# An attention and MLP-mixer kernel: the second MLP product by seven half products, keys and values pair-summed on the way in, and new step plans

## The chip, the core and the metric

The kernel runs on one core of a Trainium2 chip. A core has five engines that work side by side, each on its own queue of instructions in order: TensorE (PE, with PEld for its weight loads), VectorE (DVE), ScalarE (ACT), GpSimd (POOL) and SyncE (SP). Data move between HBM and the on-chip memory SBUF by DMA; TensorE writes its results into PSUM, eight banks of 128 rows by 2 KB. The time is device microseconds (us) of one execution. The kernel before takes 284.99 us, the median of 3 runs (284.35 to 285.2).

## The reference

Eight batches, eight heads, 576 rows, 64 columns a head (512 in all). Keys and values are averaged over groups of eight rows, so each head has 72 pooled keys. The attention output `x` goes through a token MLP with a residual, then a channel MLP with a residual:

```
k_p = k.reshape(B, H, Sp, pool, D).mean(axis=3)          # v_p likewise; pool = 8, Sp = 72
attn = softmax(scale * q @ k_p.T);  x = attn @ v_p         # -> (B, 576, 512)
h = relu(x.T @ w_tok1) @ w_tok2                            # 576 -> 256 -> 576, along the rows
u = x + h.T
h2 = relu(u @ w_ch1) @ w_ch2                               # 512 -> 1536 -> 512, along the columns
out = u + h2
```

## The kernel before

**Units.** The channel MLP is cut into nine units of 512 rows. Units 0 to 7 hold the first 512 rows of batches 0 to 7 (four chunks of 128); the last 64 rows of every batch are gathered in `u_tails`, and unit 8 takes these. In a unit (`unit_steps`, L439) the first stage makes 12 tiles of `GT` (hidden channels by rows): four matmuls of 512 columns each (L451), then a ReLU on ScalarE (L455). The second stage makes four output chunks: 12 matmuls each of 512 columns, accumulated in one bank (L474), then VectorE adds `u` (L479) and SP stores it (L482). In unit 8 the last chunk is made in two halves of 256 columns (L463).

**Steps.** `unit_steps` is a generator that yields after every two matmuls, 48 steps (0 to 47) a unit, 24 in the first stage. At a yield, `unit` (L515) issues what the plan lists for that step, so that attention work for later batches is woven between the MLP's matmuls. The order on every engine is the order of issue, written out by hand in the plans `FIRST` (unit 0), `SECOND`, `THIRD` and `LATER` (units 3 to 8), L489 to L501. A name alone is for the next batch, `<` for the unit's own batch, `>` for the batch after the next; `l` loads. Before unit 0 stands `HEAD` (L487), the attention of batch 0, in which `d` issues matmuls on zeros that keep TensorE running.

**The names in the plans.** `lk2` loads keys of batch n+2 (`lq`, `lv` likewise): one DMA from POOL's queue that casts float32 to bf16 (L87, L104). `K0`, `K1`, `V0`, `V1` pool half the heads' keys or values on POOL; `k1`, `v1` do it on VectorE: three additions (L146, L147, L150 or L152). `kpT` transposes pooled keys on TensorE and copies them to `kD` on VectorE (L195, L197). `Q0`, `Q1` transpose the queries on VectorE (L244). `s0` to `s3` are scores, eight small matmuls (L255) and two exponentials on ScalarE (L261). `av0` to `av4` make the `x` tiles: eight matmuls (L293), then a reciprocal and a product on VectorE (L305, L311). `at0`, `at1` are the token MLP's first stage, five matmuls (L339) and a ReLU, the first on ScalarE (L330), the second on VectorE (L332). `u0` to `u4` are its second stage and the residual (L354, L355), `t0` to `t4` the transposes of `u` for the next unit (L364, L365). From batch 4 on these transposes go through DRAM instead (`M`, `T`: L373 to L394).

**PSUM.** `ps_one` has three banks (first and second stage, AT, u), `ps_tr` one (transposes), `ps_two` two pairs (scores, x tiles).

## Time and profile before

| | before |
|---|---|
| median of 3 runs | 284.99 us (284.35 to 285.2) |
| the profiled execution | 285.26 us; span 283.5, so 1.76 around it |
| granted TensorE clock | 0.999 |
| head (before the first first-stage matmul) | 0 to 24.95 us |
| units 0, 1, 2 | 34.98, 32.87, 32.50 us |
| units 3, 4, 5, 6 | 28.15, 29.44, 28.59, 26.06 us |
| units 7, 8 (no attention work) | 21.24, 20.92 us |
| last matmul's end to the end of the span | 3.8 us |

The unit times are from one first-stage start (L451) to the next unit's. A line of the groups gives source line, engine, operation, output <- input, shape and count, then busy us, mean ns of one, and the idle time of the engine in front with what ended it. A line of a timeline or of the chain in order of time begins with its start and length in us. Matmuls overlap: their mean duration is longer than the distance from one start to the next, and the distance is what a row of them costs.

### The profile page before, as it was taken

How to read it: one execution, taken by the hardware profiler on the slowest of the kernel's cores; microseconds unless marked ns; L12 is line 12 of the kernel's file. 1: busy time of each engine (PE TensorE's matmuls, PEld its weight loads, DVE VectorE, ACT ScalarE, POOL GpSimd, SP SyncE). 2: the span in 40 equal slices, each digit the busy share in tenths (PEclk: the TensorE clock that was granted, in tenths of full speed). 3: DMA queues.
4: the chain of work that ended last, by engine and by line, in shares of the span. 5: the costliest groups of instructions: out<-in, count | busy, mean ns of one | idle time of the engine just before them, and what ended most of it. 6: DMA issues, size and time to landing. Idle time of an engine off the chain costs nothing.

```text
span 283.5 us, 4515 instructions
## 1 busy us (share of the span) xinstructions
PE 274.8 (97%) x1816; PEld 130.3 (46%) x1816; DVE 138.2 (49%) x265; ACT 110.3 (39%) x193; POOL 140.1 (49%) x124
## 2 busy tenths in 40 slices
PE   8999899999999999999999999999999999999994
PEld 3755335444553544354445443544354444444443
DVE  5466977777583756175247434833383141011012
ACT  2543481029404642604751366046603512612600
POOL 8584894999999939974993796000000000000000
PEclk9999999999999999999999999999999999999999
DMA  7999999960893187159649955325132445015014
GB/s 148 194 202 207 204 205 200 234 135 2 123 166 74 39 118 132 43 96 202 143 90 151 222 139 81 82 58 129 39 76 56 126 78 112 3 37 111 2 39 110
DMA packets 36837, 32.68 MB, mean 115 GB/s; under 512 B 14288, under 2 KB 30288, under 8 KB 36816
## 3 DMA queue, kind: packets, MB, share of 16 engines
q0 software_dynamic: 18672, 17.64, 39.2%
q1 hardware_dynamic: 17984, 14.62, 21.9%
q8 instruction: 14, 0.23, 0.3%
q10 hardware_dynamic: 160, 0.13, 0.2%
q14 instruction: 7, 0.06, 0.1%
HBM read 38.21 MB, written 11.80 MB: 176 GB/s over the span
## 4 chain that ended last, share of the span: by engine, by line
PE 91%; DVE 5%; ACT 2%; issue 1%
PE p L451 31%; PE p L474 31%; PE p L354 6%; PE p L339 5%; PE p L255 4%; PE p L293 3%; PE pt L508 3%; ACT ex L261 2%; PE pt L364 1%; DVE t L146 1%; PE p L463 1%; PE p L273 1%; PE p L322 1%; DVE qD L244 1%; PE p L411 1%; PE p L226 1%
## 5 line engine op out<-in xcount | busy, mean ns | idle before, releaser
L474 PE MATMUL p<-w_ch,GT 128*128 128x512 bf16 x420 | 102.3, 379 | 0.0
L451 PE MATMUL p<-uT,w_ch 128*128 128x512 bf16 x384 | 96.6, 383 | 0.0
L455 ACT ACTIVATE GT<-p 128x512 bf16<-128x512 f32 x108 | 64.3, 596 | 82.4 <-PE p L451 82.4
L451 PEld LDWEIGHTS <-w_ch 128*128 128x128 bf16 x432 | 39.8, 97 | 48.9 <-issue 4.1
L474 PEld LDWEIGHTS <-GT 128*128 128x128 bf16 x420 | 37.6, 98 | 41.4 <-issue 3.7
L261 ACT ACTIVATE ex<-p 72x576 bf16<-72x576 f32 x56 | 33.1, 642 | 26.1 <-PE p L255 26.1
L479 DVE TENSOR_TENSOR o<-p,u 128x512 f32<-128x512 f32 x32 | 21.9, 684 | 36.6 <-PE p L474 36.6
L146 POOL TENSOR_TENSOR t<-kr 72x1024 f32<-72x1024 bf16 x13 | 27.9, 2143 | 23.6 <-DMA kr<-in_k_dram 23.0
L147 POOL TENSOR_TENSOR t<-t 72x512 f32<-72x512 f32 x25 | 33.5, 1339 | 2.0
L355 DVE TENSOR_TENSOR u<-p,x 128x512 bf16<-128x512 f32 x32 | 22.1, 690 | 14.0 <-PE p L354 13.9
L146 POOL TENSOR_TENSOR t<-vr 72x1024 f32<-72x1024 bf16 x12 | 25.5, 2122 | 1.1 <-DMA vr<-in_v_dram 0.4
L311 DVE TENSOR_TENSOR x<-p,den 128x512 bf16<-128x512 f32 x30 | 20.7, 691 | 1.0
L330 ACT ACTIVATE AT<-p 128x512 bf16<-128x512 f32 x8 | 4.8, 597 | 39.4 <-PE p L339 36.6
L293 PEld LDWEIGHTS <-ex 72*128 72x128 bf16 x320 | 15.4, 98 | 9.9 <-DVE x L311 0.8
L354 PE MATMUL p<-AT,w_tok 128*128 128x512 bf16 x64 | 19.0, 378 | 0.0
L387 DVE STREAM_TRANSPOSE uT<-v 128x256 uint32<-128x256 uint32 x16 | 6.1, 419 | 24.6 <-DMA v<-mem 24.6
L293 PE MATMUL p<-vp,ex 72*128 72x65 bf16 x320 | 16.8, 194 | 0.5 <-DVE x L311 0.3
L255 PE MATMUL p<-qD,kD 32*72 32x288 bf16 x224 | 14.4, 298 | 0.7 <-DVE kD L197 0.4
L339 PE MATMUL p<-x,w_tok 128*128 128x512 bf16 x56 | 14.4, 379 | 0.0
L305 DVE RECIPROCAL den<-p 128x8 f32<-128x8 f32 (+1 forms) x39 | 8.0, 204 | 11.5 <-PE p L293 10.9
L150 POOL TENSOR_TENSOR kp<-t 72x256 bf16<-72x256 f32 x13 | 12.1, 928 | 1.0
L332 DVE TENSOR_SCALAR AT<-p 128x512 bf16<-128x512 f32 x8 | 5.5, 691 | 13.9 <-PE p L339 13.1
(88 smaller groups left out, 209.5 us busy)
## 6 DMA issues: line engine op xcount, KB each, us to landing
out_dram<-o SPq DMA_DIRECT2D x70, 128.0 KB, 2.4
kr<-in_k_dram POOLq DMA_DIRECT2D x7, 576.0 KB, 8.3
qb<-in_q_dram POOLq DMA_DIRECT2D x7, 576.0 KB, 11.7
vr<-in_v_dram POOLq DMA_DIRECT2D x7, 576.0 KB, 14.8
w_ch<-in_moe_w_ch_dram POOLq DMA_DIRECT2D x6, 512.0 KB, 13.3
mem<-u SPq DMA_DIRECT2D x8, 256.0 KB, 3.0
v<-mem SPq DMA_DIRECT2D x8, 160.0 KB, 3.8
v<-mem SPq DMA_DIRECT2D x8, 128.0 KB, 3.3
```

What stands on the lines that cost most here:

```text
L146: eng.tensor_tensor(out=t4[:, 0:n], in0=t[:, hs, 0:4], in1=t[:, hs, 4:8], op=ALU.add)
L147: eng.tensor_tensor(out=t4[:, 0:n, 0:2], in0=t4[:, 0:n, 0:2], in1=t4[:, 0:n, 2:4], op=ALU.add)
L255: nc.tensor.matmul(out=pss[l // 2][0:SP, l % 2, 0:SH], lhsT=st["kD"][quad, g, db, :], rhs=st["qD"][quad, g, half * SH:(half + 1) * SH, db] ...
L261: nc.scalar.activation(out=exv[:, h:h + 2], in_=pss[a][0:SP, :, 0:SH], func=AF.Exp, scale=scale)
L293: nc.tensor.matmul(out=halves[h // 4][:, (h % 4) * (D + 1):(h % 4 + 1) * (D + 1)], lhsT=st["ex"][:, h * S + n0:h * S + n0 + P], rhs=st["vp ...
L339: nc.tensor.matmul(out=ps, lhsT=w_tok1[:, c if c < 4 else 4 + par, m * P:(m + 1) * P], rhs=st["x"][:, c, :] if c < 4 else st["xt"], start= ...
L354: nc.tensor.matmul(out=ps, lhsT=w, rhs=a, start=(i == 0), stop=(i == len(mms) - 1))
L355: nc.vector.tensor_tensor(out=dst, in0=ps, in1=x, op=ALU.add)
L451: nc.tensor.matmul(out=ps, lhsT=w_ch1[:, kk, m * P:(m + 1) * P], rhs=blocks[kk], start=(kk == 0), stop=(kk == 3))
L455: nc.scalar.activation(out=GT[:, m, :], in_=ps, func=AF.Relu)
L474: nc.tensor.matmul(out=ps, lhsT=GT[:, m, c * P:(c + 1) * P], rhs=w_ch2[:, m, :], start=(m == 0), stop=(m == NM - 1))
L479: nc.vector.tensor_tensor(out=o_sb, in0=ps, in1=(u_tails if n == B else st["u"])[:, c, :], op=ALU.add)
```

## The change

**Seven half products.** The second stage of units 1 to 8 multiplies 512 rows x 1536 by 1536 x 512. It is cut in two along rows, hidden channels and output columns, which gives eight products of quarter size; the change makes the four output blocks out of seven such products, after Winograd's form of Strassen's scheme. With A the ReLU outputs (`GT`; first index the half of the rows, second the half of the channels) and W the weights, it forms `S0 = A21 + A22`, `S1 = S0 - A11`, `S2 = A11 - A21`, `S3 = A12 - S1` in every unit (`g_sums`, two parts a and b of 128x768 each: tokens such as `=1a` to `=4b` in the plans, where 1, 2, 3, 4 are S0, S1, S2, S3), and four sums of weights once, at the start of unit 1 (`weight_sums`, eight operations). All are on VectorE in bf16. Each product is 12 matmuls of 256 columns with a yield after every four, so a unit has 45 steps, 24 to 44 in the second stage, three a product. Products 1, 4 and 7 accumulate in one bank (`x`), 3 and 6 in another (`z`); between them VectorE reads the partial results into float32 tiles (`s1`, `s2`, `s5`, `s4`) and from these makes the output: eight evictions of 128x512 a unit for four. In unit 8 `x` is split over two banks and the last stores go out by halves.

**Loads.** Keys and values of batches 4 to 7 come as float32, in four DMAs for one: `lk`/`lv` copy two of every eight rows, then the tokens `+k3a`, `+k3b`, `+k3c` (and `+v..`) each add the next two onto them in SBUF. Each adds where the one before wrote, so it waits for it. Pooling of half the heads is then one addition instead of three.

**The rest.** Every plan is new, with the same attention work in the same unit. The second ReLU of `at` is on ScalarE for batches 1 to 7. Transposes share `ps_one`, now four banks. Two chunks are stored by one DMA per row half (four of 256 KB for eight of 128 KB), from two buffers of 128x1024 instead of four of 128x512. `qf`, `f2` and the zeros of `d` lie in one tile `area2`, `kpz`, `kT` and `qT0` in `area`; S and the weight sums take these two over from unit 1 on. `aw1` in `HEAD` is what `av1` did there before (its division on ScalarE).

```diff
+FIRST = {0: "<u1", 7: "<u0", 8: "lv2", 10: "k1 Q0", 13: "K0", 14: "kpT", 15: "s0 lk3", 16: "V0 <u2", 17: "s1 Q1",
+         19: "v1", 20: "s2", 22: "s3", 23: "<u3", 24: "lq3 av1", 25: "av0", 26: ">K0", 27: "av2 av4", 29: "av3",
+         32: "at0 at1", 33: "u4 u1", 35: "u0", 37: "u3", 41: "t0 u2", 42: ">K1", 44: "t2 t1", 47: "t3 >V0 lv3 t4"}
+SECOND = {5: "kpT", 6: "Q1", 11: "s2", 12: "Q0", 14: "lk3 v1 s0", 15: "lv3", 16: ">Q1 >K0", 17: "av1 +k3a",
+          18: "=1a", 19: "+v3a >Q0", 20: "s3", 22: "av0 >K1 +k3b lq3", 24: "s1 =2a", 25: "+v3b =1b =3b",
+          27: "av2 >V0 +k3c", 28: "av3", 29: ">V1", 30: "av4", 32: "=2b at1 =4b =3a at0", 33: "=4a >kpT", 34: "u1",
+          35: ">s0", 38: "u3 >s3", 39: "u2", 40: "t1", 41: "u0 >s2", 42: "t2 +v3c t3", 43: "t0", 44: ">s1"}
+THIRD = {0: ">Q1", 2: "lk3", 6: ">Q0", 7: "av2 av4", 8: ">K0", 10: "av0 >K1 lv3", 11: "av1", 13: ">kpT av3",
+         15: "=3b", 17: "lq3 at0", 18: ">s2", 19: "at1 =1a", 20: "=2a =3a", 21: "u3 >V0", 23: "+k3a", 24: "u0 u1",
+         25: "=1b >s0", 26: "+v3a =2b", 27: ">V1", 28: "t0 +k3b >s1", 30: "t3 >av0", 31: "=4a", 32: "t1",
+         33: ">s3 +v3b +k3c", 34: "=4b", 35: "u2", 38: ">av2", 39: "u4 >av3 t2", 41: ">av1", 42: ">av4 +v3c",
+         43: "t4"}
+LATER = {0: "lv3 >Q0 lk3", 1: "at0 at1", 3: "u4 >K0 u2", 4: ">K1 u3 +v3a", 5: "u0 +k3a", 6: ">V0 M4", 7: "lq3",
+         8: ">Q1 u1", 13: ">kpT", 16: "=3b", 18: "M2 >s0", 20: "=1a M0", 22: "=3a", 23: "+v3b >s1 M", 24: "=2a =4a",
+         25: "=1b =2b", 27: "=4b", 28: ">s3", 30: "T0", 31: "T2", 32: ">s2", 33: "T3 T1 +k3b", 34: ">V1", 35: ">av3",
+         37: ">av2", 39: ">av0", 40: ">av1 +k3c", 43: ">av4", 44: "+v3c T4"}
+LAST = {14: "=3b", 16: "=3a", 21: "=1a", 22: "=2a", 23: "=1b", 24: "=2b", 25: "=4a", 33: "=4b"}
...
+    def add_rows(b, key):
+        i = parts_of[b, key]
+        parts_of[b, key] = i + 1
+        src = (k if key == "k" else v)[b].rearrange("h (j i) d -> j h (i d)", i=POOL)
+        nc.gpsimd.dma_start(out=pair_sums(b, key), in_=src[:, :, 2 * i * D:2 * (i + 1) * D],
+                            accum_op=ALU.add if i else ALU.bypass)
...
+                i0, i1 = pair[0], pair[1]
...
+                eng.tensor_tensor(out=dst, in0=i0, in1=i1, op=ALU.add)
...
-            if m == 0:
+            if m == 0 or not first:
                 nc.scalar.activation(out=late("AT")[:, m, :], in_=ps, func=AF.Relu)
...
+    def g_sums(s):
+        S4, f, sec = fast["S"], *sums("ab".index(s[1]))
+        if s[0] == "3":
+            sub(S4[:, 2, f], GT[:, f, lo], GT[:, f, hi])
+        elif s[0] == "1":
+            nc.vector.tensor_tensor(out=S4[:, 0, f], in0=GT[:, f, hi], in1=GT[:, sec, hi], op=ALU.add)
+        elif s[0] == "2":
+            sub(S4[:, 1, f], S4[:, 0, f], GT[:, f, lo])
+        else:
+            sub(S4[:, 3, f], GT[:, sec, lo], S4[:, 1, f])
...
+        def product(ps, a, w, start, after, split=False):
+            for i in range(2):
+                for m in range(NH):
+                    nc.tensor.matmul(out=ps[i] if split else ps[:, i], lhsT=a(m)[:, i * P:(i + 1) * P], rhs=w(m),
+                                     start=start and m == 0 and (i == 0 or split), stop=(m == NH - 1),
+                                     skip_group_check=True)
+                    if (i * NH + m) % 4 == 3 and (i, m) != (1, NH - 1):
+                        yield
+                if split:
+                    after(i)
+            if not split:
+                after(slice(0, 2))
+            yield
...
+        yield from product(x, lambda m: GT[:, m, lo], lambda m: w_ch2[:, m, lo], True,
+                           plus(s1, x, u1[:, :, lo]), last)
+        yield from product(y, lambda m: GT[:, NH + m, lo], lambda m: w_ch2[:, NH + m, lo], True, plus(oa[:, :, lo], y, s1))
...
+        yield from product(z, lambda m: SG[:, 0, m], lambda m: TW[:, 0, m], True, plus(s5, z, u2[:, :, hi]))
...
+        yield from product(x, lambda m: SG[:, 1, m], lambda m: TW[:, 1, m], False,
+                           plus(s2, x, u1[:, :, hi]), last)
+        if not last:
...
+            yield from product(w, lambda m: GT[:, NH + m, hi], lambda m: TW[:, 3, m], True, plus(s4, w, u2[:, :, lo]))
+        yield from product(z, lambda m: SG[:, 3, m], lambda m: w_ch2[:, NH + m, hi], False, plus(oa[:, :, hi], z, s2))
+        store(n, 0, oa)
...
+            def finish(i):
+                plus(ob[:, :, hi], x, s5)(i)
+                plus(ob[:, :, lo], x, s4)(i)
+            yield from product(x, lambda m: SG[:, 2, m], lambda m: TW[:, 2, m], False, finish)
+            store(n, 1, ob)
```

## The prediction

> **What bounds the kernel now.** I read the page's busy shares and its chain first, then the same chain in order of time, then single lines, windows by unit and timelines where the change touches them.
>
> ```profile
> PE 274.8 (97%) x1816; PEld 130.3 (46%) x1816; DVE 138.2 (49%) x265; ACT 110.3 (39%) x193; POOL 140.1 (49%) x124
> ...
> PE 91%; DVE 5%; ACT 2%; issue 1%
> ```
>
> TensorE is the bound, over the whole span and in the chain that ended last. The end of that chain in order of time (start, length, engine, tile, line, count) shows units 7 and 8, which have no attention work mixed in:
>
> ```profile
> 248.59 10.36 PE p L474 x48
> 258.95 10.36 PE p L451 x48
> 269.31 7.77 PE p L474 x36
> 277.08 2.63 PE p L463 x24
> ```
>
> 48 second-stage matmuls of 512 columns take 10.36 us, 0.216 us each, and nothing stands between them. The last row is the form that the change uses everywhere, 256 columns. Its instructions (duration min/median/max, first and last start):
>
> ```profile
> L463 PEld LDWEIGHTS <-GT x24: 98/98/98, 276.7 to 279.3; 128*128 128x128 bf16 x24
> L463 PE MATMUL p<-w_ch,GT x24: 272/272/273, 276.9 to 279.4; 128*128 128x256 bf16 x24
> ```
>
> 24 starts in 2.5 us: 0.109 us from one to the next, although each is preceded by a weight load of 0.098 us. The loads are hidden.
>
> Windows of units 1 to 4 and unit 7 (time; busy us and count of PE, PEld, DVE, ACT, POOL; clock; DMA share; GB/s):
>
> ```profile
> 59.93:92.80 32.87, 32.14 (x245) 14.44 (x243) 21.52 (x36) 15.27 (x28) 31.37 (x24) 1.00 0.51 91
> 92.80:125.30 32.50, 31.93 (x257) 15.86 (x255) 18.39 (x41) 13.63 (x23) 26.41 (x23) 1.00 0.49 86
> 125.30:153.45 28.15, 28.15 (x191) 12.81 (x190) 13.75 (x29) 12.27 (x21) 19.82 (x16) 1.00 0.78 143
> 153.45:182.89 29.44, 29.44 (x195) 13.15 (x194) 15.05 (x32) 12.29 (x21) 16.72 (x12) 1.00 0.70 139
> 237.54:258.78 21.24, 21.24 (x97) 9.31 (x96) 2.76 (x4) 7.16 (x12) 0.00 (x0) 1.00 0.23 51
> ```
>
> PE fills every window, the clock is full, and VectorE has room, least in unit 1 (21.52 of 32.87).
>
> **The change, part by part. 1. Seven half products.** A unit's second stage goes from 48 matmuls of 512 columns to 7 x 12 = 84 of 256: 10.36 us against 84 x 0.109 = 9.16, a gain of 1.20 on the path; eight units, 9.6 us. This holds if each weight load stays hidden. The Trainium skill ("TensorE: Matmul & The Clock Gate", Part 3, "The mechanism") says that a weight load overlaps a running matmul only if it goes to other row groups. By that, 84 x (0.109 + 0.098) = 17.4 us a unit, 7 us worse than now; the row of L463, full-height loads under full-height matmuls, says otherwise and decides.
>
> **2. VectorE.** Each fast unit adds eight sums of 128x768 bf16, eight evictions of 128x512 for four, and hands one ReLU to ScalarE; unit 1 also makes eight weight sums of that size. No row has such a sum. Nearest rows:
>
> ```profile
> L365 DVE COPY uT<-pt 128x512 bf16<-128x512 bf16 x12 | 5.0, 420 | 2.4 <-PE pt L364 2.4
> L311 DVE TENSOR_TENSOR x<-p,den 128x512 bf16<-128x512 f32 x30 | 20.7, 691 | 1.0
> L300 DVE TENSOR_TENSOR x<-p,den 128x256 bf16<-128x256 f32 x2 | 0.8, 424 | 0.1
> ```
>
> L311 and L300 give a fixed 0.157 us and 1.04 ns an element: 768 elements would take 0.96 us. The copy L365, all bf16, takes half as much per element: 0.157 + 768 x 0.514 ns = 0.55. I take 0.55, since the sum is all bf16 like the copy, and keep both ends. Beside POOL it is dearer. VectorE's pooling v1 (first three rows) and POOL's K pooling (last two), from the two timelines:
>
> ```profile
> 62.89 2.01 DVE L146 TENSOR_TENSOR t<-vr 72x1024 f32<-72x1024 bf16 x1
> 64.94 1.21 DVE L147 TENSOR_TENSOR t<-t 72x512 f32<-72x512 f32 x1
> 66.18 2.23 DVE L152 TENSOR_TENSOR vp<-t 72x256 bf16<-72x256 f32 x1
> ...
> 63.90 1.70 POOL L150 TENSOR_TENSOR kp<-t 72x256 bf16<-72x256 f32 x1
> 65.68 2.45 POOL L146 TENSOR_TENSOR t<-kr 72x1024 f32<-72x1024 bf16 x1
> ```
>
> By the slope above v1 alone would be 1.22 + 0.69 + 0.42 = 2.3 us; it took 5.45. The ends alternate: each engine's operation finishes only after the other's. So a sum beside POOL waits some 1 us; between 0 and 2.12 (POOL's longest alone).
>
> Units 3 to 6: VectorE 13.75 to 15.05 + 4 x 0.69 - 0.69 + 8 x 0.55 = 20.2 to 21.5 of about 27 us (unit 6 has less), and POOL's pooling there falls to one 0.84 us operation a half. The first sum that TensorE waits for is part b of S0, behind the last ReLU of the first stage; products 1 and 2 give it 24 x 0.109 = 2.6 us against 0.2 + 0.60 + 2 x 0.55. Evictions crowd the end of a unit: after product 4 VectorE has five evictions (0.69) and five x tiles (0.9), 8.0 us, for nine steps (0.436) and five x tiles (0.26) on TensorE, 5.2; but the next unit opens with first-stage tiles that find two banks free. I take 0.1 a unit, 0.6 for units 2 to 6 with 0.2 for unit 2; 0 to 2.5. Units 7 and 8 alone have room: 0.
>
> **3. Unit 1** is the tight one. VectorE: 21.52 + 2.76 - 0.69 + 16 x 0.55 = 32.4, less 3.1 because v1 now runs while POOL waits for a buffer that v1 frees: 29.3. TensorE: 32.87 less 1.20, less about 1.0 of waits that the window holds: 30.7. 95% on a queue in order cannot be met without waits. Walking the plan: weight sums hold VectorE for the first 4.4 us, so Q1 ends 0.7 late for s2 at step 11; s0 at 14 leaves ScalarE too little before av1 at 17 (0.7); the five x tiles queue among sums that meet POOL's keys of batch 3, at1 waits 0.7 for the last; sums 2b, 4b, 3a at 32 stand before the kD copy for the next scores at 35 (0 to 2, I take 1.5). 3.6 in all, less the 1.0 of before: +2.6 against before; range -1 to +7.
>
> **4. Unit 0.** Two u's (0.43 each) leave the steps ahead of kpT, which waits for POOL (the first wait below), so that wait grows by 0.86. u4 comes one step after at1 instead of three, 0.2. t3 stands at step 47 behind the last eviction and its copy is needed by unit 1's first matmul: 0.2 + 0.69 + 0.42 less the transposes' 0.44, 0.85. Sum +1.9; 0 to 3.
>
> ```profile
> PE pt L195 <- POOL kp L150: 1.1, 1, 1.1
> ```
>
> **5. Adding DMAs.** Batches 4 to 7: four quarter loads for one, 24 more issues on POOL at 0.8 us each (L87), 19 us, against 16 poolings that fall from 4.2 to 0.84 us, 54 off; POOL is nowhere the path. Each adding load waits in POOL's queue for the one before, and pooling, the q load and the next key load queue behind. An unloaded whole load:
>
> ```profile
> kr<-in_k_dram POOLq DMA_DIRECT2D x1, 576.0 KB, 7.2
> ```
>
> A quarter should land sooner; adding is not in the trace. Bounds: 2.1 us (the u spill of 256 KB at its quickest) and 16.0 (a v load behind k and q); I take 5, between the first and the whole load. In the plan of units 3 and 4, +k3b stands at step 33, +k3c at 40, and kpT at 13 of the next unit, some 15.6 us later (11 steps of 0.436 and five x tiles of 0.26, then 13 steps of 0.43, two AT tiles of 1.08 and four u's of 0.43); two landings and 1.7 of pooling fit up to 7 us. Cost 0.
>
> **6. Rest.** Stores: four of 256 KB for eight; two buffers, landing 2.4 us, a unit apart: 0. The ReLU on ScalarE: 0.60 with 12 of 28 us busy: 0, unless exponentials delay at's. PSUM: first-stage and second-stage tiles and transposes share four banks; x and z are held through a unit, two remain: counted above. The head issues the same work: 0; if f2, qf and warm in one tile were ordered as a whole, the head would wait some 9 us for f2 (8.9 to land), but other tiles are already written in slices while read.
>
> Sum: -9.6 + 1.9 + 2.6 + 0.6 = -4.5 us. The profiled execution took 285.26 (span 283.5 and 1.76 around it), 0.27 above the median: 280.8 there, 280.5 against the median of 284.99.
>
> **Rivals.** B, the new plan's waits stay hidden (sums meet POOL little, units 0 and 1 lose 1 us together): 276.4. For it: in units 2 to 8 I find hardly a wait. Against: 95% in unit 1. C, sums at one element a cycle, 0.96: unit 1's VectorE 35.9, plus waits on POOL 3.5, against 30.7, so +8.7 for +2.6, and 2 more in units 2 to 6: -9.6 + 1.9 + 8.7 + 2.5 = +3.5, 288.5, slower. It decides from about 0.8 us a sum. For it: every two-input row on VectorE runs at that pace; against: every such row has a float32 operand. The Trainium skill ("VectorE: DVE Perf Modes", the perf-mode tier table) gives 1224 ns for 2048 bf16 elements of this operation, an estimate of 0.56 for 768; no run here shows it. D, adding loads land late: from 7 us each, units 4 and 5 wait 2 x (L - 7) each; at 9 us +8.0, 288.5; it crosses no change at 8.1. For it: runs of 512 bytes and a read of the target; against: a quarter of the bytes on a half idle queue.
>
> **How the numbers follow.** Forecast 0.50 (278 to 284), B 0.28 (275 to 278), C 0.10, D 0.08, something unseen 0.04. Range 275.3 to 287.0 leaves out the worse halves of C and D and a little of B. A measurement can tell 0.3% (0.9 us) from no change. Faster: the forecast, B and the mild ends of C and D, 0.83; same 0.03; slower 0.14.
>
> **What would show it.** Second-stage starts 0.109 us apart, 9.2 us a product set in units 7 and 8; sums of 0.55 us, longer beside POOL; unit 1 near 34 us with waits of PE on VectorE; a longer wait of kpT on POOL in unit 0; adding loads landing under 7 us. Wrong, if matmuls of 256 space wider than 0.12 in a long run, sums near 0.96, or kpT of units 2 to 5 waiting for POOL.

## The result and the profile after

The changed kernel takes 299.75 us, the median of 4 runs (297.69 to 304.9), against 285.0 for the kernel before, run beside it: a ratio of 1.0497, with a 95% interval of 1.0426 to 1.0569. It is 5% slower; the ratio leaves out the one execution of 304.9 us, which was in a slow state. The profiled execution took 298.73 us with a span of 296.8; its own surroundings add 1.9, so the span has grown by 13.3 us.

Four lines of the page of the kernel after: TensorE's and the other engines' busy shares, the granted clock in 40 slices, POOL's DMA queue (packets, MB, share of the 16 DMA engines' span), and the shares of the chain that ended last.

```profile
PE 270.7 (91%) x2092; PEld 159.1 (54%) x2092; DVE 196.5 (66%) x364; ACT 114.2 (38%) x200; POOL 119.0 (40%) x116
...
PEclk9999979999977999999999799999999999999998
...
q0 software_dynamic: 32112, 22.40, 52.3%
...
PE 72%; DVE 15%; DMA 9%; SPq 1%; issue 1%; ACT 0%; DVEq 0%
```

TensorE has less to do (270.7 us for 274.8) and yet fills only 91% of the span. In the chain its share fell from 91 to 72%; VectorE holds 15% of it and, new, DMA 9%. The clock digits are no longer all 9. POOL's queue carries 32112 packets where it carried 18672, and 22.40 MB where it carried 17.64.

The end of the chain in order of time (start, length, engine, tile, line, count), units 7 and 8:

```profile
251.62 10.88 PE p L501 x48
262.50 9.17 PE p L573 x84
271.67 10.36 PE p L501 x48
282.03 9.21 PE p L573 x84
```

L573 is the half product, L501 the first stage. 84 matmuls take 9.17 us, 0.109 each, with a weight load before every one: the saving itself is there, within a hundredth of the 9.16 that was forecast.

Windows of units 0, 1, 2, 3 and 7 (time; busy us and count of PE, PEld, DVE, ACT, POOL; clock; DMA share; GB/s):

```profile
25.43:64.84 39.41, 34.48 (x223) 15.63 (x222) 24.66 (x37) 12.72 (x23) 26.83 (x21) 0.96 1.03 170
64.84:105.41 40.57, 33.34 (x278) 18.87 (x278) 38.23 (x53) 16.04 (x28) 32.02 (x26) 0.92 0.68 106
105.41:135.50 30.09, 30.09 (x294) 19.32 (x291) 22.93 (x49) 13.94 (x24) 14.21 (x14) 1.00 0.88 141
135.50:167.99 32.49, 28.88 (x228) 17.20 (x226) 20.54 (x43) 12.76 (x22) 13.17 (x13) 0.95 0.97 155
251.46:271.51 20.05, 20.05 (x135) 12.89 (x133) 10.07 (x17) 7.17 (x12) 0.00 (x0) 1.00 0.20 54
```

Units 2 and 7 are full of TensorE work and shorter than before. Units 0, 1 and 3 are not full. In unit 1 VectorE is busy 38.23 of 40.57 us: it is the bound there. The clock is under 1 in units 0, 1 and 3, which have waits (unit 4 has waits too and keeps 1.00).

In the next table the units are measured as in the one before the prediction, from one first-stage start to the next; the head and the end from the span's borders. The forecast column is the sum of the prediction's own terms (for units 1 to 8 the 1.20 saved and what was charged against it).

| | before | after | change | forecast | missed by |
|---|---|---|---|---|---|
| head | 24.95 | 25.43 | +0.5 | 0 | 0.5 |
| unit 0 | 34.98 | 39.41 | +4.4 | +1.9 | 2.5 |
| unit 1 | 32.87 | 40.57 | +7.7 | +1.4 | 6.3 |
| unit 2 | 32.49 | 30.09 | -2.4 | -1.0 | -1.4 |
| units 3, 4 | 57.60 | 63.87 | +6.3 | -2.2 | 8.5 |
| units 5, 6 | 54.65 | 52.09 | -2.6 | -2.2 | -0.4 |
| units 7, 8 | 42.15 | 39.76 | -2.4 | -2.4 | 0 |
| after the last matmul | 3.79 | 5.61 | +1.8 | 0 | 1.8 |

So the gain did not fail to come. It came, 7.4 us in units 2 and 5 to 8, and 20.7 us were lost in the head, in units 0, 1, 3 and 4 and at the end. TensorE's longest waits (for what; us in total, times, longest) name the places:

```profile
PE p L345 <- DVE x L363: 5.6, 4, 2.3
PE p L247 <- POOL kp L193: 3.9, 1, 3.9
PE p L573 <- DVE s L594: 3.4, 2, 2.1
PE p L307 <- DVE kD L249: 2.7, 2, 2.5
```

The second is unit 0, the third is units 3 and 4, and the last is nearly all unit 1 (2.5). The first is shared: 2.3 in unit 1 and 1.5 each in units 3 and 4. These rows alone are not the loss; in units 0, 1 and 3 matmuls at half pace follow the waits, as the last section shows.

**Unit 0.** The timelines of POOL and VectorE around the pooling of batch 1's keys (start, length, engine, line, operation; in brackets the idle time before it and what ended it):

```profile
30.38 0.85 POOL L113 DMA_DIRECT2D vr<-in_v_dram  x1 [3.94 <-PE p L406]
31.24 2.13 POOL L189 TENSOR_TENSOR t<-kr 72x1024 f32<-72x1024 bf16 x1
...
29.95 0.69 DVE L407 TENSOR_TENSOR u<-p,x 128x512 bf16<-128x512 f32 x1 [2.69 <-PE p L406]
30.56 3.90 DVE L189 TENSOR_TENSOR t<-kr 72x1024 f32<-72x1024 bf16 x1
```

The load `lv2` at step 8 stands in POOL's queue ahead of `K0`, and it waits 3.94 us for TensorE's `u0` at step 7. So POOL's pooling begins at 31.24 where it began at 28.97 before. VectorE's half of the keys (`k1`) stands behind the eviction of the same `u0`, starts a moment earlier, and the two poolings then wait for each other. `kpT` waits 3.9 us where it waited 1.1.

**Unit 1.** Sums alone and beside POOL, from the two timelines:

```profile
68.58 0.55 DVE L544 TENSOR_TENSOR area<-w_ch,area 128x768 bf16<-128x768 bf16 x1
...
79.49 3.30 DVE L544 TENSOR_TENSOR area<-area,GT 128x768 bf16<-128x768 bf16 x1
...
93.62 3.57 DVE L544 TENSOR_TENSOR area<-GT,area 128x768 bf16<-128x768 bf16 x1
...
79.08 3.29 POOL L189 TENSOR_TENSOR t<-kr 72x1024 f32<-72x1024 bf16 x1
...
94.12 2.64 POOL L189 TENSOR_TENSOR t<-vr 72x1024 f32<-72x1024 bf16 x1
```

The first row is the last weight sum, made while POOL waits. The others are the same size and take six times as long, and each ends just after a pooling of POOL. The eight sums of unit 1 took 1.04, 3.30, 1.61, 1.19, 1.25, 1.50, 1.08 and 3.57 us, 14.5 for 8 x 0.55 = 4.4. Over the whole kernel 60 sums overlap no addition of POOL (median 0.55 us) and 12 overlap one (median 1.22, mean 1.60, longest 3.57). Not every operation of VectorE suffers so. The two source rows below give min/median/max in ns:

```profile
L544 DVE TENSOR_TENSOR area<-GT,area x16: 547/548/3567, 91.2 to 286.6; 128x768 bf16<-128x768 bf16 x16
```

```profile
L594 DVE TENSOR_TENSOR s<-p,u x28: 650/684/692, 85.4 to 269.1; 128x512 f32<-128x512 f32 x28
```

The evictions of L594 read one operand from PSUM. Eleven of L594's rows (outputs included) overlap an addition of POOL and have a median of 0.68 us, as those that do not. What waits is the operation with both operands in SBUF. The two longest sums have a second cause: the addition of POOL beside each was itself long (3.29 and 2.64 us for 2.1), and in unit 1 with the plain second stage (below) POOL's additions at the same places take 3.29, 3.29 and 2.65 us with no sum near them, each just behind the issue of an adding load. The Trainium skill ("SBUF — State Buffer", "Who interferes with whom") has contention only on a shared pair of ports, which it calls an exclusive lock, and names an operation of VectorE with two SBUF inputs against an instruction of GpSimd that reads SBUF. The rows agree.

**Units 3 and 4.** From the chain in order of time, the end of unit 4:

```profile
178.22 8.24 DMA mem<-u
...
188.08 4.56 DMA v<-mem
193.54 0.57 DVE s L594
194.11 0.67 DVE uT L439 x2
194.79 0.58 DVE s L594
195.51 0.70 DVE x L363
```

`u` goes to DRAM (`M`, the spill) and comes back transposed (`T`). The spill took 8.24 us to land, then the way back 4.56. VectorE's transposes L439 wait for it at the head of VectorE's queue, and behind them stand evictions that TensorE needs: `s` (L594), then the x tiles (L363). The page's DMA groups (KB each, median us from issue to landing) and the wait:

```profile
kr<-in_k_dram POOLq DMA_DIRECT2D x16, 288.0 KB, 7.4
mem<-u SPq DMA_DIRECT2D x8, 256.0 KB, 5.4
```

```profile
DVE uT L439 <- DMA v<-mem: 9.0, 2, 4.9
```

In units 3 and 4 the spills landed after 8.2 to 10.4 us, where the kernel before had 3.8 to 6.9; in unit 5, where no load is left, after 2.1 and 2.5. VectorE waited for `v<-mem` before the change too, 24.6 us in all:

```profile
DVE uT L387 <- DMA v<-mem: 24.6, 4, 7.9
```

But after the head TensorE then waited for VectorE 0.5 us at the longest: nothing that it needed soon stood behind that wait.

### The profile page after: what moved, and what is told of

Its sections match the earlier page's. It is cut to its first block, busy times and chain, and to the rows that moved or that the text cites. A ratio compares the mean times of both kernels' runs of the same rounds, so it can differ in the third digit from the quotient of the medians.

```text
span 296.8 us, 5196 instructions
## 1 busy us (share of the span) xinstructions
PE 270.7 (91%) x2092; PEld 159.1 (54%) x2092; DVE 196.5 (66%) x364; ACT 114.2 (38%) x200; POOL 119.0 (40%) x116
## 3 DMA queue, kind: packets, MB, share of 16 engines
q0 software_dynamic: 32112, 22.40, 52.3%
## 4 chain that ended last, share of the span: by engine, by line
PE 72%; DVE 15%; DMA 9%; SPq 1%; issue 1%; ACT 0%; DVEq 0%
PE p L501 25%; PE p L573 20%; DMA mem<-u 6%; PE p L406 6%; DVE area L544 5%; PE p L391 4%; PE p L524 3%; PE p L345 3%; DMA v<-mem 3%; PE p L648 3%; PE p L307 2%; DVE t L189 2%; DVE s L594 1%; DVE x L363 1%; DVE vp L195 1%; SPq L432 1%
## 5 line engine op out<-in xcount | busy, mean ns | idle before, releaser
L501 PE MATMUL p<-uT,w_ch 128*128 128x512 bf16 x384 | 94.9, 386 | 0.7 <-DVE uT L417 0.7
L501 PEld LDWEIGHTS <-w_ch 128*128 128x128 bf16 x432 | 40.4, 98 | 49.9 <-issue 4.3
L573 PEld LDWEIGHTS <-area 128*128 128x128 bf16 x384 | 36.8, 101 | 11.8 <-issue 5.1
L573 PE MATMUL p<-area,area 128*128 128x256 bf16 x288 | 38.8, 281 | 1.2 <-DVE area L551 1.2
L126 POOL DMA_DIRECT2D kr<-in_k_dram x16 | 23.1, 1443 | 30.5 <-DMA kr<-in_k_dram 30.5
L126 POOL DMA_DIRECT2D vr<-in_v_dram x16 | 23.1, 1550 | 24.7 <-DMA vr<-in_v_dram 14.9
L573 PEld LDWEIGHTS <-GT 128*128 128x128 bf16 x288 | 26.8, 98 | 6.8 <-issue 2.3
L594 DVE TENSOR_TENSOR o<-p,s 128x512 f32<-128x512 f32 (+1 forms) x32 | 20.8, 668 | 6.0 <-PE p L573 5.8
L573 PE MATMUL p<-w_ch,GT 128*128 128x256 bf16 x192 | 23.8, 273 | 0.0
L551 DVE TENSOR_TENSOR area<-GT 128x768 bf16<-128x768 bf16 x16 | 11.5, 721 | 15.8 <-ACT GT L505 15.8
L594 DVE TENSOR_TENSOR s<-p,u 128x512 f32<-128x512 f32 x28 | 19.0, 679 | 4.1 <-PE p L573 4.0
L363 DVE TENSOR_TENSOR x<-p,den 128x512 bf16<-128x512 f32 x30 | 20.7, 692 | 1.0
L544 DVE TENSOR_TENSOR area<-GT 128x768 bf16<-128x768 bf16 x16 | 11.3, 709 | 10.2 <-ACT GT L505 10.2
L573 PE MATMUL p<-w_ch,area 128*128 128x256 bf16 x96 | 13.7, 278 | 3.4 <-DVE s L594 3.4
```

The lines of the kernel that those rows point to most:

```text
L126: nc.gpsimd.dma_start(out=pair_sums(b, key), in_=src[:, :, 2 * i * D:2 * (i + 1) * D], accum_op=ALU.add if i else ALU.bypass)
L363: nc.vector.tensor_tensor(out=dst.rearrange("p (a h d) -> p a h d", a=2, d=D), in0=view[:, :, :, 0:D], in1=den[rows, :, :, None].broadcast ...
L501: nc.tensor.matmul(out=ps, lhsT=w_ch1[:, kk, m * P:(m + 1) * P], rhs=uT[kk], start=(kk == 0), stop=(kk == 3))
L544: nc.vector.tensor_tensor(out=out, in0=a, in1=b, op=ALU.subtract)
L573: nc.tensor.matmul(out=ps[i] if split else ps[:, i], lhsT=a(m)[:, i * P:(i + 1) * P], rhs=w(m), start=start and m == 0 and (i == 0 or spli ...
L594: nc.vector.tensor_tensor(out=out[:, i], in0=ps[i] if type(ps) is list else ps[:, i], in1=other[:, i], op=ALU.add)
```

## The experiments

Unit times of the profiled executions, in us, for all of them. A run for which one time alone is given is a single execution; the kernel after alone ranged from 297.69 to 300.77 us, so a microsecond or two in the total of such a run says little.

| | head | 0 | 1 | 2 | 3 | 4 | 5 | 6 | 7 | 8 | end | span |
|---|---|---|---|---|---|---|---|---|---|---|---|---|
| before | 24.95 | 34.98 | 32.87 | 32.49 | 28.15 | 29.45 | 28.59 | 26.06 | 21.24 | 20.91 | 3.79 | 283.5 |
| after | 25.43 | 39.41 | 40.57 | 30.09 | 32.49 | 31.38 | 27.30 | 24.79 | 20.05 | 19.71 | 5.61 | 296.8 |
| no adding loads | 25.18 | 38.41 | 37.68 | 31.27 | 32.24 | 28.16 | 27.30 | 24.56 | 20.05 | 19.71 | 5.62 | 290.2 |
| unit 1 plain | 25.23 | 38.53 | 31.45 | 36.67 | 35.77 | 31.75 | 27.30 | 24.56 | 20.05 | 19.71 | 5.62 | 296.6 |
| old order in unit 0 | 25.34 | 34.86 | 42.92 | 30.09 | 30.34 | 35.96 | 27.51 | 24.56 | 20.05 | 19.71 | 5.64 | 297.0 |
| transposes last | 25.17 | 38.59 | 40.57 | 30.09 | 30.68 | 34.34 | 31.17 | 29.35 | 20.06 | 19.71 | 5.61 | 305.3 |
| quarters not added | 25.58 | 38.76 | 40.59 | 30.09 | 36.27 | 28.16 | 27.30 | 24.79 | 20.05 | 19.71 | 5.61 | 296.9 |
| last stores by whole rows | 25.10 | 38.54 | 40.56 | 30.09 | 32.66 | 31.26 | 27.30 | 24.78 | 20.05 | 19.71 | 4.99 | 295.0 |
| products from unit 4 | 25.04 | 36.10 | 31.77 | 31.67 | 36.90 | 34.78 | 27.30 | 24.79 | 20.05 | 19.71 | 4.93 | 293.0 |
| adding loads alone | 25.37 | 34.85 | 31.77 | 31.67 | 30.05 | 40.26 | 37.90 | 25.97 | 21.23 | 20.88 | 5.55 | 305.5 |
| from unit 4, old loads | 25.32 | 33.90 | 32.00 | 31.65 | 28.96 | 29.75 | 27.30 | 24.56 | 20.05 | 19.71 | 5.49 | 278.7 |
| from unit 2, old loads | 25.25 | 34.69 | 32.00 | 43.75 | 27.50 | 28.16 | 27.30 | 24.56 | 20.05 | 19.71 | 5.48 | 288.4 |
| from unit 1, old loads | 25.39 | 34.38 | 53.22 | 31.88 | 27.50 | 28.16 | 27.30 | 24.56 | 20.05 | 19.71 | 5.46 | 297.6 |
| units 3 to 7, sums spread | 25.41 | 33.17 | 31.77 | 31.67 | 33.29 | 29.07 | 27.30 | 24.79 | 20.05 | 20.91 | 3.80 | 281.2 |
| units 5 to 7 | 25.20 | 35.82 | 31.77 | 31.67 | 28.93 | 29.36 | 27.30 | 24.79 | 20.05 | 20.91 | 3.80 | 279.6 |

The table shows two more things. Units 6 and 7 with eight products and the old plans (adding loads alone) take 25.97 and 21.23 us, with seven 24.79 and 20.05: a product set is worth 1.18 us. And units 1 and 2 with the old plans and eight products take 31.8 to 32.0 and 31.7 us in these kernels, 0.8 to 1.1 less than before, without a product in them. That must come from what else of the change stays in them (such as four shared banks, the second ReLU of `at` on ScalarE, pairs stored together); no run separates these.

### Without the adding loads

```diff
-SUMMED = 4
+SUMMED = 8
```

> Keys and values of all batches are loaded by one casting load and pooled by three additions, as before; all else is the changed kernel. Theory (adding loads hold the DMA engines, the spill through DRAM lands late, and its transposes block VectorE's queue): in units 3 and 4 the u spill lands in 4 to 7 us instead of 10, the waits of TensorE there (3.9 and 3.1 us) fall below 1, the two units take 27.5 to 29 us each instead of 32.5 and 31.4; unit 1 keeps most of its 9.6 us of waits. Total 291 to 294 us. Rival (VectorE is overloaded by sums and evictions, with POOL's longer pooling on top): units 3 and 4 stay at 31 us or more, total 298 or more.

One execution took 292.09 us; the span is 6.6 under that of the kernel after. The total fits the theory; unit 3 does not, it is at the rival's 31 or more. The tail of the spill is gone from unit 4 (31.38 to 28.16), and unit 1 gains 2.9. Unit 3 stays where it was: with the whole pooling back on POOL, its sums now meet POOL instead, and TensorE waits 2.0 us in one place for a sum. So without the adding loads about half of the 13.3 us is gone; the other half stays with the plan and the sums.

### Unit 1 with the plain second stage

The weight sums move to the start of unit 2.

```diff
-        if n == 1:
+        if n == 2:
...
-        for i, _ in enumerate((unit_fast if n >= 1 else unit_plain)(n, st)):
+        for i, _ in enumerate((unit_fast if n >= 2 else unit_plain)(n, st)):
...
-                    g_sums(s[1:])
+                    if n >= 2:
+                        g_sums(s[1:])
```

> Unit 1 keeps the second stage of eight products (48 matmuls of 512 columns, four evictions, no sums); the seven products begin with unit 2, and the weight sums stand at its start. Theory (unit 1 loses its time because sums on VectorE meet POOL's pooling): unit 1 falls from 40.6 to 33 to 35 us although its second stage is 1.2 us longer; unit 2 grows by 0 to 2 us; total 291 to 294. Rival (unit 1's new order of steps is at fault, not the sums): unit 1 stays above 38 us, total 297 or more.

298.54 us in one execution, against the 291 to 294 of the theory. Windows of units 1 and 2:

```profile
63.76:95.21 31.45, 31.17 (x237) 14.41 (x242) 18.56 (x33) 17.21 (x30) 24.84 (x19) 1.00 0.70 119
95.21:131.88 36.67, 32.07 (x287) 20.24 (x290) 29.40 (x56) 12.88 (x22) 21.65 (x22) 0.91 0.84 127
```

Unit 1 falls from 40.57 to 31.45 us, under the 32.87 of before: its loss comes with the products in it (sums, weight sums and evictions together), since the same plan and the same loads without them cost nothing. But unit 2, which now holds the weight sums, rises by 6.6, where 0 to 2 were expected, and unit 3 by 3.3. The loss moved.

### The old order of steps in unit 0

`FIRST` is that of the kernel before.

```diff
-FIRST = {0: "<u1", 7: "<u0", 8: "lv2", 10: "k1 Q0", 13: "K0", 14: "kpT", 15: "s0 lk3", 16: "V0 <u2", 17: "s1 Q1",
+FIRST = {0: "<u0 K0 lv2 V0", 1: "<u1", 2: "<u2", 3: "<u3 k1", 7: "Q0 Q1", 14: "kpT v1",
...
```

> Unit 0 runs by the plan of before (u2, u3, the v load of batch 2 and the pooling placed as they were); all else is the changed kernel. Theory (POOL's and VectorE's pooling of batch 1's keys start late behind a load and an eviction, and TensorE has less work ahead of kpT, then runs at half clock): unit 0 falls from 39.4 to 35 to 36 us, its wait for kpT from 3.9 to 1 to 1.5 us, and the second matmul row after it goes at full pace; total 294 to 296. Rival (the new order of allocations of PSUM or the loads make unit 0 slow): unit 0 stays above 38 us.

298.88 us in one execution, where 294 to 296 were expected. Unit 0 goes back to 34.86 us and `kpT` waits 1.4 instead of 3.9: the order of these steps is what cost unit 0 its 4.4 (in the table above unit 0 takes 33.2 to 36.1 us in the eight experiments with the old order, and 38.4 to 39.4 in the six kernels with the new). But unit 1 gives 2.4 us back and unit 4 4.6, while unit 3 gains 2.2, and the sum does not move. Why was not followed; that the loads and poolings behind unit 0 now fall on other moments of the later units is a guess.

### The transposes of units 3 to 8 at the unit's end

```diff
-         25: "=1b =2b", 27: "=4b", 28: ">s3", 30: "T0", 31: "T2", 32: ">s2", 33: "T3 T1 +k3b", 34: ">V1", 35: ">av3",
-         37: ">av2", 39: ">av0", 40: ">av1 +k3c", 43: ">av4", 44: "+v3c T4"}
+         25: "=1b =2b", 27: "=4b", 28: ">s3", 32: ">s2", 33: "+k3b", 34: ">V1", 35: ">av3",
+         37: ">av2", 39: ">av0", 40: ">av1 +k3c", 43: ">av4", 44: "+v3c T0 T2 T3 T1 T4"}
```

> In units 3 to 8 the five transposes T of the spilled u move from steps 30 to 44 to the last step, behind all x tiles on VectorE's queue; the loads stay as changed. Theory (the transposes wait for a late DMA at the head of VectorE's queue and the evictions of the product banks stand behind them): the waits of TensorE inside the second stage of units 3 and 4 (3.9 and 3.1 us) go; since the transposes then end a unit, 1 to 2.5 us come back at the start of units 4 to 7 each where the next first stage waits for them. Total 296 to 300, with units 3 and 4 at 28 to 30 us. Rival (VectorE has too much to do there whatever its order): the waits in units 3 and 4 stay at 3 us or more.

307.25 us in one execution, 8.5 more, where 296 to 300 were expected. The waits inside the second stages of units 3 and 4 go, as the theory of evictions behind the transposes has it, and a new one takes their place:

```profile
PE p L501 <- DVE uT L439: 13.6, 4, 3.7
```

The next unit's first matmuls (L501) wait for the transposes, four times, 3.4 us on average, for the 1 to 2.5 expected. Two of the four are at the starts of units 6 and 7, behind spills that landed in 2.1 to 2.7 us; so transposes at the end hold up the next unit even when the spill is quick. Neither of the two places tried is free: in the middle evictions stand behind the transposes, at the end the next unit does.

### Quarter loads that don't add

```diff
-                            accum_op=ALU.add if i else ALU.bypass)
+                            accum_op=ALU.bypass)
```

> The quarter loads of batches 4 to 7 stay, with the same sizes, order and waits, but each overwrites the one before instead of adding onto it, so three quarters of these keys and values are left out of the result. Theory (the adding itself makes the loads slow, since the target is read too): a later quarter takes 0.8 us to issue instead of 1.4 to 2.0 and lands in 4 to 5.5 us instead of 5.6 to 12, the spill of unit 3 lands in 5 to 7 us instead of 10, units 3 and 4 lose at least 3 us together, total 290 to 295. Rival (the number of loads and their 512-byte runs are at fault): issue and landing stay within 15%, units 3 and 4 stay above 31 us.

298.81 us in one execution, as with the adding, where 290 to 295 were expected. For the 24 quarters that add, the issue on POOL falls from 1.4 to 2.0 us to 0.81 to 0.85, and the landing from 5.6 to 12.6 us (median 7.2) to 4.2 to 10.0 (median 5.2). So adding makes a quarter load dearer. But the time does not come back. Unit 4 is clean (28.16): its last quarter had landed at 169.7 us, before the unit began, and the spill took 2.1. In unit 3 the way back of `u`, issued at 149.7 to 151.1, landed 6.5 to 11.7 us later among the loads of that moment, and TensorE waited for one eviction behind it:

```profile
PE p L573 <- DVE s L594: 5.8, 1, 5.8
```

Here the price of one transfer fell and the total stayed: which transfers meet weighed as much.

### The last stores by whole rows

```diff
-                               plus(ob[:, :, hi], x, s5, store_part(hi)), True)
+                               plus(ob[:, :, hi], x, s5), True)
...
-                               plus(ob[:, :, lo], x, u2[:, :, lo], store_part(lo)), True)
+                               plus(ob[:, :, lo], x, u2[:, :, lo], store_part()), True)
```

> The last unit stores its second pair of chunks in four transfers of whole rows after the last sum instead of eight of half rows. Theory (the end is longer because SP issues six stores in a row): from the last matmul's end to the end of the span 3.5 to 4.0 us instead of 5.6, total lower by 1.6 to 2.0. Rival (larger transfers land later, or the store of the first pair is what ends last): 5 us or more.

296.82 us in one execution; the end shrinks from 5.61 to 4.99 us, 0.6 of the 1.8, which is where the rival put it (the theory said 3.5 to 4.0). Fewer stores are issued, but the larger ones (128 KB) land after 3.2 to 3.6 us where the last three of 64 KB took 2.0 to 2.3. With the second stage of the kernel before in unit 8 (the last two experiments) the end is 3.8 again.

### Products from unit 4 on, no adding loads

The plans of the kernel before in units 0 to 3, the new `LATER` from unit 4.

```diff
-SUMMED = 4
+SUMMED = 8
...
-PLANS = {0: FIRST, 1: SECOND, 2: THIRD, 8: LAST}
+PLANS = {0: FIRST, 1: SECOND, 2: THIRD, 3: BEFORE, 8: LAST}
...
+        for i, _ in enumerate((unit_fast if n >= 4 else unit_plain)(n, st)):
```

> Plans of before in units 0 to 3 with the second stage of eight products, no adding loads, the seven products in units 4 to 8 only (where POOL has little or nothing to pool), and the four whole-row stores at the end. Theory (the products themselves gain 1.2 us a unit wherever VectorE does not meet POOL and no transfer is late): units 0 to 3 as before (128.5 us together), units 4 to 8 each 1.2 to 1.5 shorter, total 278.5 to 280.5, ratio 0.977 to 0.985. Rival (the shared PSUM banks, the single store buffers or the sums cost about what the products gain wherever they stand): 283 to 287.

294.72 us, a ratio of 1.0355 (1.0295 to 1.0416) to the kernel before: slower, against what was expected. Units 1, 2 and 5 to 8 do as expected; unit 3, which has the old plan and no product in it, takes 36.90 for 28.15. VectorE's wait in it, behind which TensorE waited 7.2 us for an x tile:

```profile
DVE uT L440 <- DMA v<-mem: 15.8, 1, 15.8
```

The new `LATER` loads keys and values at step 0, ahead of the pooling in POOL's queue. POOL thus ran a unit ahead: the loads for unit 4's step 0 were issued at 125.7 and 126.5, in unit 3, right behind those of unit 3 itself (123.3 to 124.9), and the spill and its way back landed after 7.4 to 9.5 us each. Those two landed after 22 us. The place of a load in POOL's queue decides when it goes out, and pooling that waits for its data is what had held the loads back. Unit 4 (34.78) lost 4.8 us to another wait, for VectorE's `u_tails`, which was not followed.

### The adding loads alone

The plans of the kernel before, eight products everywhere, adding loads at the steps of the change.

```diff
-        for i, _ in enumerate((unit_fast if n >= 1 else unit_plain)(n, st)):
+        for i, _ in enumerate((unit_fast if n >= 99 else unit_plain)(n, st)):
...
+         14: "u0", 15: "u1", 17: "u2 t0", 18: "u3", 19: "t1 u4", 21: "t2", 23: "t3 +k3a", 25: "t4 >kpT", 26: ">Q1 +v3a",
+         27: ">s0", 28: "+k3b", 29: ">s1", 32: ">s2", 33: "+v3b +k3c", 35: ">s3", 38: ">av0", 40: ">av1", 42: ">av2 +v3c", 44: ">av3", 46: ">av4"}
```

> The kernel before in its plans and its eight products everywhere, with the adding loads of batches 4 to 7 placed at the steps that the change gives them, and pairs stored together. Theory (adding loads hold the DMA engines so that the spill lands late, which costs only where work that TensorE needs stands behind the transposes): spill of units 3 and 4 lands in 8 to 11 us; TensorE waits 0 to 3 us in units 3 and 4, total 285 to 289. Rival (adding loads are slow only beside the change's own traffic): spill in 5 to 7 us, no waits, 284 to 286.

307.29 us in one execution, 22 more than before and far over both forecasts, all of it in units 3 to 5:

```profile
PE p L248 <- POOL kp L242: 16.5, 4, 8.3
```

Here four landings in a chain hold up the pooled keys themselves, the mechanism of the prediction's rival D. The spill did not land late: it took 3.0 to 4.6 us, for the theory's 8 to 11. In the kernel after it is the other way round: from batch 2 on no wait of TensorE is for pooled keys, and the spill is late. So these loads cost in different ways under the two plans, and this run does not price them in the other.

### Products with the old loads: from unit 4, 2 and 1

The three kernels load whole keys and values behind the pooling, as before. Units without products have the old plans, the others the tokens for the sums added.

```diff
+LATER = {0: ">K0 >K1 >V0 >V1 lk3 lq3 lv3 >Q0", 1: "at0 at1", 3: "u4 u2", 4: "u3", 5: "u0", 6: "M4",
+         8: ">Q1 u1", 13: ">kpT", 16: "=3b", 18: "M2 >s0", 20: "=1a M0", 22: "=3a", 23: ">s1 M", 24: "=2a =4a",
+         25: "=1b =2b", 27: "=4b", 28: ">s3", 30: "T0", 31: "T2", 32: ">s2", 33: "T3 T1", 35: ">av3",
+         37: ">av2", 39: ">av0", 40: ">av1", 43: ">av4", 44: "T4"}
```

> Kernel: the loads, the plans and the plain second stage of the kernel before in units 0 to 3; seven products in units 4 to 8 (the weight sums at the start of unit 4); keys and values of all batches loaded whole, at the places in POOL's queue where the kernel before loads them, that is behind the pooling and not ahead of it; the upper halves of unit 8's columns stored once for both row chunks. Theory (the products are worth 1.2 to 1.3 us in every unit where the sums don't meet POOL's pooling and where no load comes near the spill of u; what was lost came from the adding loads, from loads issued ahead of the pooling and from sums beside POOL): units 0 to 3 as in the kernel before (35, 32, 32, 28 to 29 us), unit 4 28 to 29 with the weight sums in it, units 5 to 8 27.3, 24.8, 20.05, 19.7, tail 4 to 5, in all 277 to 282 us, faster than the kernel before by 1 to 3%. Rival (the shared PSUM banks and the eight evictions for four cost what the products save, whatever the loads do): units 4 to 6 at or over 29.4, 28.6, 26.1, in all 283 to 287.

> Kernel: as the products from unit 4 with whole loads, but seven products from unit 2 on (weight sums at the start of unit 2). The eight sums of units 2 and 3 now fall beside POOL's full pooling (three additions a half). Theory of sums beside POOL: each pair of a sum and a pooling addition costs VectorE 1 to 3.6 us for 0.55, so units 2 and 3 give the 1.2 us back or more: 31.5 to 35 and 28 to 30 us, in all 0 to 4 us above the products from unit 4. Rival (POOL's company costs TensorE nothing outside unit 1, because units 2 and 3 leave VectorE enough room): both units 1 to 1.3 us under the kernel before, in all 2 to 2.5 us below the products from unit 4.

> Kernel: as before, seven products from unit 1 on (weight sums at the start of unit 1), whole loads at their old places everywhere. It is the product part of the change without its loads. Theory: unit 1, where VectorE is nearly full, loses 2 to 8 us against the kernel before by sums and poolings that wait for one another, though no adding load is there; units 2 and 3 as in the run with products from unit 2; in all 282 to 290 us. Rival (the losses of unit 1 came from the change's own step plan or its loads, not from sums beside POOL): unit 1 at 30.5 to 33 us, in all 276 to 280.

From unit 4: 282.79 us, ratio 0.9895 (0.9845 to 0.9946), 1% faster than before, just over the range of 277 to 282; unit 4, at 29.75 us, is over its 28 to 29. Against the earlier run from unit 4 little but the order of loads and poolings in POOL's queue is changed, and unit 3 is at 28.96 for 36.90, unit 4 at 29.75 for 34.78. The rival (the products' costs elsewhere eat their gain) falls for units 5 to 8, which save 1.2 to 1.5 us each.

From unit 2: 292.48 us, ratio 1.0294 (1.024 to 1.0348), 9.7 above the run from unit 4, more than the 4 expected. Unit 3 gains 0.65 against the kernel before and unit 4 1.3. The whole loss, 11.3 us, is in unit 2, where eight weight sums stand in a row in front of the x tiles while POOL pools values: TensorE waits 6.4 us for an x tile, and later 3.0 for a copy that stands behind unit 2's own sums.

From unit 1: 300.19 us, ratio 1.0532 (1.0499 to 1.0565), slower than forecast and as slow as the change itself, without one adding load. Unit 1 loses 20 us. Its weight sums meet POOL's pooling of keys:

```profile
61.62 2.35 DVE L547 TENSOR_TENSOR area<-w_ch,area 128x768 bf16<-128x768 bf16 x1
```

```profile
PE p L310 <- DVE qD L299: 10.8, 1, 10.8
```

The eight took from 60.75 to 72.1, 11.4 us instead of the 4.05 of the kernel after (65.09 to 69.14), and the queries' transposes behind them (L299) kept TensorE waiting 10.8. This says something for the plan of the change: it had placed its weight sums where POOL waits (0.55 us each), and only the other eight met POOL in its unit 1.

### Is it the sum or the place: units 3 to 7, and units 5 to 7

Both kernels use the same plan `SUMS` in the first unit with products; the weight sums come one at a time. Unit 8 has the old second stage.

```diff
+SUMS = dict(LATER)
+for step, i in {6: "0a", 7: "0b", 8: "1a", 9: "1b", 10: "3a", 11: "3b", 12: "2a", 14: "2b"}.items():
+    SUMS[step] = SUMS.get(step, "") + " =w" + i
+PLANS = {0: FIRST, 1: SECOND, 2: THIRD, 3: SUMS}                        # units 3 to 7
+PLANS = {0: FIRST, 1: SECOND, 2: THIRD, 3: BEFORE, 4: BEFORE, 5: SUMS}  # units 5 to 7
```

> Kernel: as the products from unit 4 with whole loads, but seven products in units 3 to 7, the eight weight sums one at a time at steps 6 to 14 of unit 3 (partly where POOL waits for the keys' load, 3 to 9.5 us into the unit, partly beside its pooling), and the plain second stage and the single stores of the kernel before in unit 8. Theory (a sum beside POOL takes 1 to 3.6 us, and that costs TensorE only where evictions that it needs soon stand behind a row of them; spread over a unit with room the sums cost little): unit 3 27.5 to 28.5 us, unit 4 28.2, units 5 to 7 27.3, 24.6, 20.05, unit 8 and tail 20.9 + 3.8; against the products from unit 4 with whole loads -1.0 to -3.5 us, in all 276 to 281. Rival (weight sums cost their unit what they cost in a row, 1.6 us or more, and products beside POOL's full pooling do not pay): unit 3 29 to 32 us, in all 280 to 285.

> Kernel: as before it, but seven products only in units 5 to 7, after POOL's last pooling; the weight sums at steps 6 to 14 of unit 5. No sum meets POOL. Theory: weight sums and sums at 0.55 us each, unit 5 27.3 us, units 6 and 7 24.6 and 20.05, units 0 to 4 and 8 as in the kernel before (35, 32.9, 32.5, 28.2, 29.5, 20.9; a little less with four shared banks), tail 3.8, in all 279 to 282 us, 1 to 2% faster than the kernel before, and with the smallest spread between runs. Rival (products cost elsewhere what they save): 283 or more.

Products in units 3 to 7 took 283.12 us in the profiled execution and 287.9 to 289.4 in three others, so that how it compares with the kernel before stays unclear and only its profile is read here. Unit 3 takes 33.29 us, worse than the 28.5 that my theory allowed and than the rival's 32. VectorE's sums in it, then POOL's additions at the same time, then the wait:

```profile
134.09 2.48 DVE L556 TENSOR_TENSOR area<-GT 128x768 bf16<-128x768 bf16 x1
136.49 1.62 DVE L563 TENSOR_TENSOR area<-GT 128x768 bf16<-128x768 bf16 x1
...
133.61 2.54 POOL L192 TENSOR_TENSOR t<-kr 72x1024 f32<-72x1024 bf16 x1 [7.41 <-DMA kr<-in_k_dram]
136.22 1.46 POOL L193 TENSOR_TENSOR t<-t 72x512 f32<-72x512 f32 x1
```

```profile
PE p L590 <- DVE area L563: 3.3, 1, 3.3
```

The two engines go in lockstep, one sum for one addition of POOL, and a product (L590) waits 3.3 us for the sum itself. The eight took 13.8 us, and behind the wait the granted clock is 0.50 from 143.4 to 150.2. No row of evictions is needed for the loss: the weight sums, spread over the steps, took 0.55 us each while POOL still waited for its load, and the sums of the unit, spread too, were late because POOL had begun. (In the run with products from unit 2, unit 3 gained although it had sums beside POOL; by its timeline only the first three of the eight met it, 2.33, 1.62 and 1.08 us, and the rest took 0.55.) In the other kernel the same sums in the same order fall in unit 5, after POOL's last pooling:

```profile
194.93 0.55 DVE L556 TENSOR_TENSOR area<-GT 128x768 bf16<-128x768 bf16 x1
195.79 0.56 DVE L563 TENSOR_TENSOR area<-GT 128x768 bf16<-128x768 bf16 x1 [0.31 <-ACT GT L508]
```

Unit 5 takes 27.30 us for 28.59, weight sums included, and the kernel 280.97 us, a ratio of 0.9885 (0.9824 to 0.9947): 1.2% faster than the kernel before, and 19 us faster than the change. With the run from unit 4 it is the only version that is shown to beat both; the two cannot be told apart. Not all of the gain is the products': units 5 to 7 give 3.75 us, units 1 and 2, which have none, 1.9.

## Why the prediction was wrong

The forecast was 280.5 us; 299.75 were measured. The saving was right. What failed is what the change costs the neighbours: sums beside POOL (step 3), evictions behind a late spill (steps 2 and 5) and the order in unit 0 (step 4).

**Step 1, seven half products: right.** 0.109 us a start, 9.17 us a set, 1.2 to 1.5 us saved in every unit without waits. The row of L463 carried over from 24 matmuls to 84.

**Step 2, VectorE: the sum right, its company mis-sized.** 0.55 us alone was the value taken, and 0.55 was measured; the rival with 0.96 falls. (The estimate of 0.56 from the Trainium skill, "VectorE: DVE Perf Modes", the perf-mode tier table, agrees.) The wait beside POOL was given as some 1 us, 0 to 2.12. Its mean in the kernel after is 1.05 (1.60 less 0.55) and its longest 3.0. The price was thus right on average; the forecast did not multiply it, and only rival C carries a sum for it, 3.5 us.

**Step 3, unit 1: the largest miss in one unit, 6.3 us.** It counted VectorE at 29.3 us with all sixteen sums at 0.55, after the step before had just priced the wait beside POOL. With the eight sums at what they took, 10.1 more, the same count is 39.4, against TensorE's 30.7; measured were 38.23 busy in 40.57. The products' saving was then lost in the one unit that the prediction itself called tight. That the loss comes with the products is shown by unit 1 with the plain second stage; that it is their sums beside POOL, by the rows of unit 1 and by the last two experiments. The adding loads have a part in it: without them unit 1 is 2.9 us shorter.

**Step 2 again, the ends of units 3 and 4: the largest miss of all, 8.5 us in two units.** It took 0.1 us a unit there. It says that VectorE has room there, and it has (20.5 busy of 32.5). What failed is the cover behind the transposes: the transposes L387 of the kernel before already waited 24.6 us for the way back of `u` and cost TensorE next to nothing, because nothing that it soon needed stood behind them. The change puts evictions of products there, and the prediction did not name what stands behind that wait.

**Step 4, unit 0: right in sign, +4.4 for +1.9.** It counted the two `u`s ahead of `kpT`, 0.86 us. It did not follow `lv2`, which was moved from step 0 to step 8 in front of `K0` and waits for `u0` (3.94 us), nor `k1` behind the eviction of that `u0`. With the old order the wait was 1.4.

**Step 5, adding loads, "cost 0": wrong by about 6.6 us.** A landing was put at 5 us with harm from 7; the medians of all quarters were 7.4 for keys and 7.7 for values, those that add took 5.6 to 12.6 us, and an issue took POOL 1.4 to 2.0 us for 0.8. The harm that was priced (late pooled keys) did not come in the kernel after; the harm that came, to the spill and through it to VectorE's queue, was not looked for. Rival D, with late loads, thus had the cause and not the way. That the loads as such cost in units 1 and 4 is shown by the run without adding; how much of unit 3 is theirs stays open, since there the sums take their place.

**Step 6, the rest: +0.5 in the head and +1.8 at the end for 0.** At the end SP issues six stores one after the other (289.33 to 293.76, the last landing 2.03 us later). Of the 1.8, 0.6 is shown to hang on their number and size, and all of it on the new second stage with its stores: with the old one in unit 8 the unit and its end take 20.91 + 3.80 = 24.7 us, with products 19.71 + 5.61 = 25.3, and with products and whole-row stores 19.71 + 4.99 = 24.7, so there the products gain nothing. The head's 0.5 was not tested.

The range of 275.3 to 287.0 took these terms as separate and small. The cases of loss that it weighed were each one mechanism of 4 to 8 us; three came together. None of the three signs of being wrong that it named came (matmuls spaced wider than 0.12, sums near 0.96, `kpT` of units 2 to 5 waiting for POOL): they watched the price of each instruction alone, and the loss lay in what stood beside and behind it.

## What to carry to other kernels

Before work is given to an engine that has room, multiply each of its instructions by its price beside the neighbour that it will really run beside: here a 0.55 us sum of two SBUF operands took some 1.2 us beside GpSimd (median) and up to 3.6, and the same sums placed after GpSimd's last pooling were worth their full gain. A long wait of an engine off the path is harmless only because of what stands behind it, so name that before putting anything new there. And a step moved in a hand-written order must be followed on every queue that it enters: a load in front of a pooling sets both when the pooling begins and what transfers meet.
